# RetNet recurrence and SwiGLU block: first loads and steps in another order, the last token block in two halves, three w_out loads in two transfers

## The chip, the cores and the metric

The kernel runs on one core of a Trainium2 chip. The metric is the device time of one execution in microseconds. Five engines matter: TensorE (PE, with its weight loads PEld), VectorE (DVE), ScalarE (ACT), GpSimd (POOL) and SyncE (SP), which issues nearly all DMAs.

## The reference

```python
batch, n_heads, seq, head_dim = (4, 8, 768, 64)          # q, k, v, float32
n_tokens, d_model, d_ff = (3072, 512, 1536)              # w_gate, w_val: 512x1536, w_out: 1536x512

gamma = 1.0 - 2.0 ** (-5.0 - np.arange(H))
for t in range(S):
    state = gamma * state + outer(k[t], v[t])            # per batch and head
    y[t] = (1 / sqrt(D)) * q[t] @ state
x = y.transpose(0, 2, 1, 3).reshape(B * S, H * D)
g = x @ w_gate
out = (g * sigmoid(g) * (x @ w_val)) @ w_out
```

## The kernel before

**Tiling.** The sequence of each batch is cut into chunks of 128 tokens, and the heads are taken in four pairs. A chunk's contribution is a masked product of scores with v, plus a product of the decayed q with the state that the chunks before left. The work goes in four segments of six chunks (three positions of two batches). For each segment the attention output becomes x, then the two up products (w_gate, w_val) give h, then the down product with w_out gives six token blocks of 128 x 512 in six PSUM banks.

Products keep more than single precision's fast mode would: each operand is split in three parts (`near_a`, `near_b`, `near_c` at L960, L963, L966; `far_a`, `far_b`, `far_c` at L969, L399/L972, L976), and each product is three matmuls, one for each part. The weights come as 64-bit words and are converted on the chip to single precision (`convert_a` L532, L535, L538 on ScalarE, `convert_b` L545 and `convert_c` L553 on VectorE). Segment 0 keeps its converted weights in DRAM for the later segments, w_out's three parts in `w_dn3`.

**Order.** Nothing is scheduled by a framework. `PLAN` is one long string of names; `run` calls the step of each name in that order, so that the string sets each engine's instruction order. Every engine takes its instructions in order and waits at the head of its queue. The names of the start, with chunk numbers n from 0 to 5 (0 and 1 are the first chunks of two batches, 2 and 3 the second, 4 and 5 the third):

- `l n:w` loads k_t (w = 0), q_t (1), v (2) or k_n (3) of chunk n, 256 KB each (L464); q_t of chunks 0 and 1 is loaded on ScalarE's queue ahead of the plan. `A0`, `A1`, `A2` load the table: the two halves of the score mask and the decay factors (L586). `U`, `V` load weights (L511, 512 KB a matrix and block, in halves for block 0: gate with `U0:0`, val with `V0:0`).
- `s n` scores on TensorE (L628) and mask on VectorE (L634); `m n` masked scores times v (L713); `o n` decayed q times the old state (L699); `t n` the state's growth (L684), copied on ScalarE (L687) for chunks 0 and 1 or added on VectorE (L689); `g n` the state's decay (L670); `k n`, `q n` scale k_n and q on GpSimd (L649, L643), `K n`, `Q n` the same on VectorE; `x n:1`, `x n:2` split the attention output into x.
- `a`, `b`, `S`, `c`, `C` convert a weight block, one step after the other on ScalarE, ScalarE, VectorE, ScalarE, VectorE; `n f:i` makes the three parts of a weight block (0 to 2 gate, 3 to 5 val); `p f:j` and `v f:j` are the gate and val products for the chunk pair j of the first two blocks (L906), `u` and `y` the activation and product behind them; `G`, `W` the products of the later blocks (L888); `Z` keeps a converted block in DRAM.

The DMA completions use eight semaphores in turn: a load is issued when the one eight places earlier, over both queues, has landed.

**The end.** In a segment's down stage, `D f.tok` is the three matmuls of weight block f for token block tok (`down`, L1117 to L1122), `W f` loads the block's three parts from `w_dn3` (`w_load`, L1104), and `e tok` scales a token block out of its bank and stores it (`finish`, L1124 to L1143): odd blocks on VectorE (L1140), even ones on ScalarE (L1142), each stored through SP in one transfer. In the last segment block 5 is done in two halves, columns 0 to 255 on ScalarE (L1134) and 256 to 511 on VectorE (L1136). The last names of the plan are `3/D10.2 3/D11.2 3/e2`: token block 2 is the last.

Of the kernel before, what the change touches and what calls it, by code (L numbers as in the profile page):

```python
# [47 lines left out]


PLAN = """  # L50
    l1:0 A2 l0:0 A1 A0 l0:2 U0:0 l2:1 l0:3 s0 a0:1 l2:0 s1 m0 K0 b0:1 V0:0 S0:1 c0:1 l1:2 x0:2 s2
    l1:3 l3:0 x0:1 C0:1 l3:1 k1 U1:1 l2:3 t0 l2:2 l4:0 a0:0 g2 n0:0 Q2 l4:1 n0:1 m1 b0:0 S0:0 c0:0
    n0:2 t1 x1:1 a1:1 l3:3 x1:2 o2 C0:0 a1:0 s3 b1:1 S1:1 l3:2 q3 l5:1 n0:3 n0:4 c1:1 p0:0 l5:2 k2
    l5:0 o3 C1:1 m2 n0:5 t2 s4 b1:0 k3 v0:0 x2:2 S1:0 u0:0 g3 l4:2 U2:0 c1:0 m3 n1:0 U12:3 x2:1 t3
    C1:0 s5 q5 n1:1 h0 q4 o5 o4 x3:1 x3:2 m4 T0:0 n1:3 y0:0 T0:1 m5 p0:1 v0:1 a2 x4:1 u0:1 x5:2 U3:1
    n1:4 T1:0 y0:1 n1:2 T1:1 b2 p1:0 T0:2 U4:0 n1:5 u1:0 a12 Z0 p1:1 a3 x4:2 v1:0 x5:1 v1:1 y1:0
    p0:2 u1:1 v0:2 S2 U5:1 b12 c2 p1:2 u0:2 S12 T1:2 y1:1 C2 n2:0 n2:3 v1:2 y0:2 Z1 b3 n2:1 u1:2
    n2:2 S3 n2:4 T2:0 c3 a4 U13:2 G2:1 C3 y1:2 U6:0 T2:1 n3:0 G2:0 b4 n2:5 n3:1 i2:0 i2:1 T2:2 c12
    W2:0 j2:0 n3:2 W2:1 G3:1 n3:3 S4 C12 a5 Z2 j2:1 Z12 n3:4 c4 C4 U7:1 n3:5 T3:0 T3:1 c13 T3:2 G3:0
    n4:0 n4:1 b5 S5 n4:2 W3:0 n4:3 W3:1 i3:0 i3:1 n4:4 a13 a6 G4:1 c5 Z3 b13 G4:0 T4:0 U8:0 C5 T4:1  # L60
    j3:1 n4:5 b6 U14:3 W4:1 n5:0 T4:2 n5:1 i4:1 n5:2 n5:3 j3:0 S6 i4:0 a7 c6 n5:4 W4:0 T5:0 C6 G5:1
    Z4 T5:1 n6:0 L U9:1 j4:0 n5:5 S13 G5:0 a8 b7 n6:3 T5:2 j4:1 n6:1 c14 C13 W5:1 S7 i5:1 Z5 n6:4
    i5:0 n6:2 j5:1 c7 W5:0 G6:1 n6:5 l4:3 a9 U10:0 C7 n7:0 G6:0 j5:0 i6:1 T6:0 k4 b8 g4 Z13 n7:1
    n7:3 U15:2 S8 n7:2 W6:1 i6:0 c8 n7:4 T7:0 a14 W6:0 C8 l5:3 T7:1 T6:1 b14 G7:1 U11:1 n8:0 n8:1
    n7:5 i7:1 T6:2 G7:0 j6:0 b9 S14 W7:0 h2 c15 j6:1 Z6 S9 C14 n8:3 c9 n8:2 i7:0 n8:4 W7:1 G8:1 T7:2
    C9 G8:0 j7:0 n8:5 a10 b10 n9:0 j7:1 n9:3 Z14 a15 W8:0 P2 W8:1 Z7 n9:4 k5 b15 i8:0 S10 T8:0 n9:1
    i8:1 U16:3 n9:5 c10 S15 P0 T8:1 n9:2 C10 a11 C15 G9:0 t4 G9:1 P1 T9:0 i9:0 T8:2 Z15 j8:1 g5 j8:0
    t5 W9:1 W9:0 b11 n10:0 U17:2 T9:1 c16 Z8 n10:3 1/was0.0 a16 i9:1 n10:1 n10:4 n10:2 b16 G10:1 S11
    n10:5 c11 S16 i10:1 G10:0 0/h0.0 j9:0 C16 Z16 C11 n11:0 W10:0 n11:3 a17 j9:1 i10:0 0/h0.1 b17
# [299 lines left out]
def tile_retnet_swiglu(  # L369
# [747 lines left out]
    def down(f, tok):  # L1117
        i, u = divmod(tok, L)
        for a in range(3):
            nc.tensor.matmul(banks[tok], hs[f][:, a, ds(i * TH + u * P, P)], wo[f][:, a],  # L1120
                             start=f == a == 0, stop=f == NF - 1 and a == 2,
                             skip_group_check=True)  # L1122

    def finish(s, tok):  # L1124
        i, u = divmod(tok, L)
        p, pos = divmod(s * L, NCK)
# [4 lines left out]
        scale = ONE * ONE
        if s == NSEG - 1 and tok == 5:
            a, b = (ds(n * DM // 2, DM // 2) for n in range(2))
            act(t[:, a], banks[tok][:, a], AF.Copy, scale=scale)  # L1134
# [1 line left out]
            nc.vector.tensor_scalar(t[:, b], banks[tok][:, b], scale, None, op0=mul)  # L1136
            nc.sync.dma_start(out=out[ds(row, P), b], in_=t[:, b])
            return
        if tok % 2:
            nc.vector.tensor_scalar(t, banks[tok], scale, None, op0=mul)  # L1140
        else:
            act(t, banks[tok], AF.Copy, scale=scale)  # L1142
# [153 lines left out]
```

## Time and profile before

| | |
|---|---|
| runs | 643.41, 645.41, 645.75 us (median 645.41) |
| profiled execution | 643.87 us; span of its instructions 642.1 us |
| TensorE busy | 632.8 us of the span, granted clock 1.00 |
| TensorE's first real matmul | 6.67 us; its last wait ends at 16.79 us |
| TensorE's last matmul ends | 638.3 us |
| last store issued, landed | 638.96, 641.0 us |
| moved by DMA | 140.13 MB, 218 GB/s over the span |

A line of the chain of waits has the start in us, the length in us, and what the end waited for. A line of the timeline has the start, the length, the engine, the line of the program, the operation, the tiles written and read, how many instructions were merged, and in brackets the idle time before it and what ended that. A single-precision matmul appears in the timeline as two passes, so a step of eight matmuls is x16; the three-part products appear as one pass each.

### The profile page before, as it was taken

How to read it: one execution, taken by the hardware profiler on the slowest of the kernel's cores; microseconds unless marked ns; L12 is line 12 of the kernel's file. 1: busy time of each engine (PE TensorE's matmuls, PEld its weight loads, DVE VectorE, ACT ScalarE, POOL GpSimd, SP SyncE). 2: the span in 40 equal slices, each digit the busy share in tenths (PEclk: the TensorE clock that was granted, in tenths of full speed). 3: DMA queues.
4: the chain of work that ended last, by engine and by line, in shares of the span. 5: the costliest groups of instructions: out<-in, count | busy, mean ns of one | idle time of the engine just before them, and what ended most of it. 6: DMA issues, size and time to landing. Idle time of an engine off the chain costs nothing.

```text
span 642.1 us, 14098 instructions
## 1 busy us (share of the span) xinstructions
PE 632.8 (99%) x5576; PEld 580.2 (90%) x5576; DVE 487.8 (76%) x712; ACT 391.8 (61%) x860; POOL 264.5 (41%) x174
## 2 busy tenths in 40 slices
PE   7999999999999999999999999999999999999997
PEld 6899999987779999997778999998777999999886
DVE  4988887999898887665787869675789866778361
ACT  3678797777865565666766555564785555654121
POOL 0625555554436875630003665550101666653000
PEclk9999999999999999999999999999999999999999
DMA  9989988789787445258775640457767444304554
GB/s 320 375 290 338 317 320 290 281 290 328 259 283 298 170 151 173 69 171 270 248 240 213 198 164 8 183 196 247 241 223 264 155 163 173 115 0 157 195 184 170
DMA packets 50050, 140.13 MB, mean 218 GB/s; under 512 B 4928, under 2 KB 17472, under 8 KB 49984
## 3 DMA queue, kind: packets, MB, share of 16 engines
q1 hardware_dynamic: 49552, 138.57, 62.7%
q8 instruction: 44, 0.72, 0.5%
q10 hardware_dynamic: 432, 0.66, 0.3%
q14 instruction: 22, 0.18, 0.1%
HBM read 109.32 MB, written 29.88 MB: 217 GB/s over the span
## 4 chain that ended last, share of the span: by engine, by line
PE 97%; DMA 2%; SPq 0%; POOL 0%; ACT 0%; issue 0%; POOLq 0%
PE bank L1057 41%; PE bank L1120 32%; PE bank L888 13%; PE bank L758 6%; PE bank L906 3%; DMA hT<-in_k_n_dram 1%; DMA tab<-in_decays_dram 1%; PE bank L713 1%; PE bank L699 1%; PE bank L628 1%; PE bank L684 0%; POOL hT L649 0%; SPq L586 0%; SPq L464 0%; ACT chunk_x L1142 0%
## 5 line engine op out<-in xcount | busy, mean ns | idle before, releaser
L1120 PE MATMUL bank<-oitem,gitem 128*128 128x512 f32 x864 | 208.5, 395 | 0.0
L1120 PEld LDWEIGHTS bank<-oitem,gitem 128*128 128x128 f32 x864 | 159.0, 188 | 35.3 <-DMA oitem<-wdnt 0.5
L966 POOL TENSOR_TENSOR gitem<-gitem 128x768 fp32r<-128x768 f32 x72 | 140.6, 1963 | 116.6 <-DVE gitem L963 98.6
L1057 PE MATMUL bank<-xa,gitem 128*128 128x384 f32 x864 | 160.5, 334 | 0.0
L1057 PEld LDWEIGHTS bank<-xa,gitem 128*128 128x128 f32 x864 | 150.8, 188 | 0.2
L966 POOL TENSOR_TENSOR oitem<-oitem 128x256 fp32r<-128x256 f32 (+1 forms) x60 | 65.7, 1102 | 53.0 <-DVE oitem L963 51.2
L1057 PE MATMUL bank<-xb,gitem 128*128 128x384 f32 x432 | 84.5, 334 | 0.0
L888 PE MATMUL bank<-xa,oitem 128*128 128x384 f32 x480 | 84.4, 335 | 0.0
L888 PEld LDWEIGHTS bank<-xa,oitem 128*128 128x128 f32 x480 | 83.0, 188 | 0.4 <-DVE hT L442 0.2
L963 DVE SCALAR_TENSOR_TENSOR gitem<-gitem,loads 128x768 fp32r<-128x768 f32 x72 | 75.1, 1058 | 9.2 <-ACT gitem L960 7.8
L1057 PEld LDWEIGHTS bank<-xb,gitem 128*128 128x128 f32 x432 | 75.9, 188 | 0.4
L960 ACT ACTIVATE gitem<-loads 128x768 fp32r<-128x768 f32 x72 | 59.6, 843 | 25.9 <-PE bank L1057 16.8
L963 DVE SCALAR_TENSOR_TENSOR gitem<-gitem,hT 128x768 fp32r<-128x768 f32 x48 | 46.2, 965 | 25.4 <-ACT gitem L960 25.4
L960 ACT ACTIVATE gitem<-hT 128x768 fp32r<-128x768 f32 x48 | 40.2, 841 | 32.4 <-PE bank L1120 30.2
L991 ACT COPY chunk_x<-bank 64x128 f32<-64x128 f32 x144 | 36.6, 260 | 31.9 <-PE bank L758 21.1
L399 DVE SCALAR_TENSOR_TENSOR gitem<-gitem 128x768 fp32r<-128x768 f32 x48 | 49.1, 1030 | 0.8
L785 POOL TENSOR_TENSOR loads<-loads,tab 128x512 f32<-128x512 f32 x9 | 13.3, 1475 | 81.7 <-PE bank L758 44.6
L1057 PE MATMUL bank<-xb,oitem 128*128 128x384 f32 x216 | 43.4, 335 | 0.0
L1057 PEld LDWEIGHTS bank<-xb,oitem 128*128 128x128 f32 x216 | 38.0, 188 | 0.3
L1074 DVE TENSOR_TENSOR hT<-bank,tmp 128x384 f32<-128x384 f32 x36 | 20.0, 554 | 20.1 <-PE bank L1057 19.9
L963 DVE SCALAR_TENSOR_TENSOR oitem<-oitem,loads 128x256 fp32r<-128x256 f32 (+1 forms) x42 | 34.1, 816 | 0.9 <-ACT oitem L960 0.8
L1072 ACT COPY tmp<-bank 128x384 f32<-128x384 f32 x36 | 17.2, 478 | 27.9 <-PE bank L1057 18.9
(112 smaller groups left out, 792.3 us busy)
## 6 DMA issues: line engine op xcount, KB each, us to landing
loads<-wup SPq DMA_DIRECT2D x36, 896.0 KB, 4.7
oitem<-wdnt SPq DMA_DIRECT2D x36, 768.0 KB, 4.4
wdnt<-oitem SPq DMA_DIRECT2D x12, 768.0 KB, 5.9
wup<-first SPq DMA_DIRECT2D x9, 896.0 KB, 5.5
rawp<-in_w_gate_dram SPq DMA_DIRECT2D x12, 512.0 KB, 6.6
rawp<-in_w_val_dram SPq DMA_DIRECT2D x12, 512.0 KB, 6.2
rawp<-in_w_out_dram SPq DMA_DIRECT2D x12, 512.0 KB, 6.8
out_dram<-chunk_x SPq DMA_DIRECT2D x22, 256.0 KB, 2.2
```

The source lines that it names most:

```text
L399: stt(o, x, 1.0, y, op0=mul, op1=op)
L758: nc.tensor.matmul(o, a, b, start=start, stop=True, skip_group_check=True)
L888: nc.tensor.matmul(o, w[:, a, ts(b, P)], X0[:, a, i, NC - 1 - b], start=a == b == 0, stop=a == 2 and b == NC - 1, skip_group_check=True)
L906: nc.tensor.matmul(o, w[:, a, ts(b, P)], X0[:, a, :, NC - 1 - b, ts(j, P)], start=a == b == 0, stop=a == 2 and b == NC - 1, skip_group_che ...
L960: act(o[0], x, AF.Copy, scale=CUT / FAR)
L963: stt(o[1], f32(o[0]), -FAR, x, op0=mul, op1=add)
L966: op(o[2], f32(o[0]), f32(o[1]), op=add)
L991: copy(cx[half[i], ds(2 * h, 2), c, half[z]], y.rearrange("p (b t) -> p b t", b=2))
L1057: nc.tensor.matmul(o, w[:, a, k], x[:, a, KH - 1 - k], start=start and a == k == 0, stop=a == 2 and k == KH - 1, skip_group_check=True)
L1072: steps = (lambda: copy(p1, x), lambda: tt(c11, z, p1, op=add), lambda: act(gate, c11, AF.Silu, scale=ONE), lambda: copy(u2, x), lambda: c ...
L1074: lambda: copy(p5, wb), lambda: tt(h1, x, p5, op=add),
L1120: nc.tensor.matmul(banks[tok], hs[f][:, a, ds(i * TH + u * P, P)], wo[f][:, a], start=f == a == 0, stop=f == NF - 1 and a == 2, skip_group ...
```

## The change

It has four parts. The first 16 lines of `PLAN` (to about 100 us of the run) are written in another order, with the same names; the rest of the plan is as it was. The start of it before and after:

```diff
 PLAN = """
-    l1:0 A2 l0:0 A1 A0 l0:2 U0:0 l2:1 l0:3 s0 a0:1 l2:0 s1 m0 K0 b0:1 V0:0 S0:1 c0:1 l1:2 x0:2 s2
-    l1:3 l3:0 x0:1 C0:1 l3:1 k1 U1:1 l2:3 t0 l2:2 l4:0 a0:0 g2 n0:0 Q2 l4:1 n0:1 m1 b0:0 S0:0 c0:0
-    n0:2 t1 x1:1 a1:1 l3:3 x1:2 o2 C0:0 a1:0 s3 b1:1 S1:1 l3:2 q3 l5:1 n0:3 n0:4 c1:1 p0:0 l5:2 k2
-    l5:0 o3 C1:1 m2 n0:5 t2 s4 b1:0 k3 v0:0 x2:2 S1:0 u0:0 g3 l4:2 U2:0 c1:0 m3 n1:0 U12:3 x2:1 t3
-    C1:0 s5 q5 n1:1 h0 q4 o5 o4 x3:1 x3:2 m4 T0:0 n1:3 y0:0 T0:1 m5 p0:1 v0:1 a2 x4:1 u0:1 x5:2 U3:1
+    l0:2 l0:0 A1 A0 l1:0 U0:0 a0:1 s0 s1 l0:3 b0:1 l2:0 l2:1 S0:1 A2 K0 m0 c0:1 l1:3 C0:1 n0:0 l1:2
+    s2 V0:0 k1 l2:3 l2:2 Q2 t0 a0:0 l3:1 b0:0 m1 l3:0 U1:1 n0:1 x0:2 S0:0 o2 x0:1 c0:0 l4:0 l4:1
+    l3:3 t1 l3:2 m2 x1:1 C0:0 n0:3 k2 x1:2 g2 n0:4 t2 s3 a1:1 l5:1 b1:1 S1:1 n0:2 p0:0 x2:2 a1:0 q3
+    n0:5 k3 c1:1 g3 C1:1 b1:0 l5:0 v0:0 s4 S1:0 h0 l5:2 o3 m3 l4:2 t3 c1:0 C1:0 U2:0 x3:2 s5 u0:0 q5
+    x2:1 q4 U3:1 o5 o4 n1:0 x3:1 n1:1 n1:3 m4 n1:4 n1:2 m5 a2 T1:0 y0:0 U12:3 x5:1 x4:1 p0:1 u0:1 b2
...
```

So SP's queue begins, before, with k_t 1, A2, k_t 0, A1, A0, v 0, gate half 0, q_t 2, k_n 0, k_t 2, val half 0, v 1, k_n 1; and after with v 0, k_t 0, A1, A0, k_t 1, gate half 0, k_n 0, k_t 2, q_t 2, A2, k_n 1, v 1, val half 0, k_n 2, v 2. TensorE's first steps are s0, s1, m0, s2, t0, m1, t1, o2, s3, p0, o3, m2, t2, s4, v0, m3, t3, s5 before, and s0, s1, m0, s2, t0, m1, o2, t1, m2, t2, s3, p0, v0, s4, o3, m3, t3, s5 after.

In the last segment the loads of the w_out blocks 0, 1 and 2 go in two transfers, the first two parts (512 KB) and the third (256 KB). The last three matmuls of token block 2 become six, three for each half of the columns, and its scaling and store go in two halves, VectorE and SP for the first, ScalarE and its queue for the second:

```diff
             else:
-                nc.sync.dma_start(out=o, in_=w_dn3[f])
+                for i in (slice(2), slice(2, 3)) if s == NSEG - 1 and f < 3 else (slice(None),):
+                    nc.sync.dma_start(out=o[:, i], in_=w_dn3[f][:, i])
...
+    halves_of = [ds(n * DM // 2, DM // 2) for n in range(2)]
+    FINAL = 2
+
-    def down(f, tok):
+    def down(s, f, tok):
         i, u = divmod(tok, L)
-        for a in range(3):
-            nc.tensor.matmul(banks[tok], hs[f][:, a, ds(i * TH + u * P, P)], wo[f][:, a],
-                             start=f == a == 0, stop=f == NF - 1 and a == 2,
-                             skip_group_check=True)
+        final = s == NSEG - 1 and f == NF - 1 and tok == FINAL
+        for cols in halves_of if final else [slice(None)]:
+            for a in range(3):
+                nc.tensor.matmul(banks[tok][:, cols], hs[f][:, a, ds(i * TH + u * P, P)],
+                                 wo[f][:, a, cols], start=f == a == 0,
+                                 stop=f == NF - 1 and a == 2, skip_group_check=True)
...
+        if s == NSEG - 1 and tok == FINAL:
+            a, b = halves_of
+            nc.vector.tensor_scalar(t[:, a], banks[tok][:, a], scale, None, op0=mul)
+            nc.sync.dma_start(out=out[ds(row, P), a], in_=t[:, a])
+            act(t[:, b], banks[tok][:, b], AF.Copy, scale=scale)
+            nc.scalar.dma_start(out=out[ds(row, P), b], in_=t[:, b])
+            return
```

In the changed kernel's own numbering the two scalings of block 2 are L1147 (VectorE) and L1149 (ScalarE), and the products are L1126.

More of the change, by code (lines that the diff above doesn't have):

```diff
@@ L56 @@
[L56 to L66, printed above, removed]
+    l0:2 l0:0 A1 A0 l1:0 U0:0 a0:1 s0 s1 l0:3 b0:1 l2:0 l2:1 S0:1 A2 K0 m0 c0:1 l1:3 C0:1 n0:0 l1:2
@@ new lines @@
+    s2 V0:0 k1 l2:3 l2:2 Q2 t0 a0:0 l3:1 b0:0 m1 l3:0 U1:1 n0:1 x0:2 S0:0 o2 x0:1 c0:0 l4:0 l4:1
+    l3:3 t1 l3:2 m2 x1:1 C0:0 n0:3 k2 x1:2 g2 n0:4 t2 s3 a1:1 l5:1 b1:1 S1:1 n0:2 p0:0 x2:2 a1:0 q3
+    n0:5 k3 c1:1 g3 C1:1 b1:0 l5:0 v0:0 s4 S1:0 h0 l5:2 o3 m3 l4:2 t3 c1:0 C1:0 U2:0 x3:2 s5 u0:0 q5
+    x2:1 q4 U3:1 o5 o4 n1:0 x3:1 n1:1 n1:3 m4 n1:4 n1:2 m5 a2 T1:0 y0:0 U12:3 x5:1 x4:1 p0:1 u0:1 b2
+    T0:0 T1:1 v0:1 T0:1 y0:1 n1:5 p1:0 x4:2 T0:2 T1:2 p1:1 v1:0 u1:0 a3 a12 u1:1 x5:2 v1:1 U4:0 p0:2
@@ new lines @@
+    b12 y1:0 v0:2 p1:2 U5:1 S2 y1:1 S12 c2 Z1 u0:2 C2 n2:0 b3 y0:2 n2:1 u1:2 n2:3 v1:2 S3 y1:2 c3 Z0
+    n2:4 n2:2 T2:0 U13:2 G2:1 a4 C3 G2:0 n2:5 T2:1 U6:0 W2:0 i2:1 T2:2 n3:0 b4 i2:0 c12 a5 n3:1 n3:2
+    j2:0 W2:1 S4 n3:3 Z2 n3:4 c4 C12 c13 Z12 G3:1 j2:1 C4 U7:1 i3:1 n3:5 n4:0 T3:0 G3:0 i3:0 n4:1
+    n4:2 n4:3 T3:1 W3:1 a13 b5 T3:2 G4:1 Z3 a6 n4:4 S5 c5 j3:1 W3:0 C5 n5:0 n4:5 G4:0 b6 b13 T4:0
+    T4:1 n5:1 L U8:0 T4:2 n5:3 U14:3 n5:2 i4:1 j3:0 S6 n5:4 W4:1 a7 W4:0 c6 i4:0 T5:0 C6 G5:1 c14
@@ L67 @@
+    n6:0 n5:5 Z4 S13 j4:1 T5:1 G5:0 n6:3 a8 W5:1 j4:0 T5:2 U9:1 n6:1 n6:2 n6:4 C13 Z5 b7 W5:0 i5:1
+    j5:1 S7 n6:5 U10:0 G6:1 i5:0 c7 C7 a9 j5:0 l4:3 G6:0 T6:0 i6:1 n7:0 b8 n7:3 g4 W6:0 l5:3 n7:1
+    Z13 U15:2 n7:2 S8 W6:1 c8 T6:1 i6:0 a14 b14 n7:4 n7:5 T7:0 G7:1 C8 T7:1 U11:1 G7:0 i7:1 n8:0
+    j6:0 n8:3 S14 W7:0 n8:1 b9 T6:2 c15 j6:1 n8:4 i7:0 S9 Z6 k4 n8:2 h2 W7:1 C14 c9 G8:1 T7:2 C9
+    G8:0 j7:0 n8:5 a10 b10 n9:0 j7:1 n9:3 Z14 a15 W8:0 P2 W8:1 Z7 n9:4 k5 b15 i8:0 S10 T8:0 n9:1
     i8:1 U16:3 n9:5 c10 S15 P0 T8:1 n9:2 C10 a11 C15 G9:0 t4 G9:1 P1 T9:0 i9:0 T8:2 Z15 j8:1 g5 j8:0
@@ L1132, in finish @@
         if s == NSEG - 1 and tok == 5:
-            a, b = (ds(n * DM // 2, DM // 2) for n in range(2))
+            a, b = halves_of
             act(t[:, a], banks[tok][:, a], AF.Copy, scale=scale)
@@ L1137, in finish @@
             nc.sync.dma_start(out=out[ds(row, P), b], in_=t[:, b])
+            return
+        if s == NSEG - 1 and tok == FINAL:
+            a, b = halves_of
+            nc.vector.tensor_scalar(t[:, a], banks[tok][:, a], scale, None, op0=mul)
+            nc.sync.dma_start(out=out[ds(row, P), a], in_=t[:, a])
+            act(t[:, b], banks[tok][:, b], AF.Copy, scale=scale)
+            nc.scalar.dma_start(out=out[ds(row, P), b], in_=t[:, b])
             return
@@ L1191, in down_stage @@
             tok = b
-            at(t, f"{s}/D{f}.{tok}", down, f, tok)
+            at(t, f"{s}/D{f}.{tok}", down, s, f, tok)
             t += 3 * PASS_D
```

## The prediction

> **What bounds the kernel now.** I read four views: the page's busy shares, the chain of waits, the timeline of TensorE's start, and the timeline of the tail.
>
> ```profile
> PE 632.8 (99%) x5576; PEld 580.2 (90%) x5576; DVE 487.8 (76%) x712; ACT 391.8 (61%) x860; POOL 264.5 (41%) x174
> ...
> PE 97%; DMA 2%; SPq 0%; POOL 0%; ACT 0%; issue 0%; POOLq 0%
> ```
>
> TensorE is the bound. In the chain nothing but TensorE stands between 16.79 and 638.32 us:
>
> ```profile
> 2.59 5.46 DMA tab<-in_decays_dram
> 8.05 0.02 issue
> 8.06 7.49 DMA hT<-in_k_n_dram
> ...
> 15.69 1.05 POOL hT L649
> 16.75 0.04 issue
> 16.79 0.69 PE bank L684 x16
> ...
> 32.80 14.59 PE bank L906 x120
> ...
> 590.66 47.66 PE bank L1120 x210
> 638.32 0.02 issue
> 638.34 0.60 ACT chunk_x L1142
> ```
>
> So time can be won or lost only before 16.79 and after 638.3, unless the new order opens a hole in between. TensorE's start:
>
> ```profile
> 6.67 3.63 PE L628 MATMUL bank<-hT 64*128 64x128 f32 x32 [1.80 <-DMA hT<-in_k_t_dram]
> 10.22 1.09 PE L713 MATMUL bank<-tmp,hT 128*64 128x128 f32 x16
> 12.84 1.16 PE L628 MATMUL bank<-hT 64*128 64x128 f32 x16 [1.52 <-DMA hT<-in_k_t_dram]
> 13.93 0.69 PE L684 MATMUL bank<-hT 128*64 128x64 f32 x16
> 14.92 1.09 PE L713 MATMUL bank<-tmp,hT 128*64 128x128 f32 x16 [0.30 <-DMA hT<-in_v_n_dram]
> ```
>
> These are s0 and s1, m0, s2, t0, m1. TensorE waits for loads four times; the last wait ends at 16.79, for the k_n of chunk 1 and the GpSimd scaling behind it. Where the last wait ends, with the work already done by then, sets everything after it.
>
> **The loads.** Each landing in the trace follows the one before it by 0.68 us per 256 KB (k_n of chunk 0 at 12.02, k_t of 2 at 12.71, v of 1 at 14.88, k_n of 1 at 15.56); a 512 KB weight half takes 1.49 (val half 0, at 14.20) to 1.95 (gate half 0, at 10.66). The first eight landings are at 4.49, 4.67, 5.55, 5.87, 6.54, 7.37, 8.05, 8.71. An issue waits until the load eight earlier has landed (the gate half was issued at 4.68, chunk 0's q_t landed at 4.67). So a load's landing follows from its place in the queue.
>
> **Part 1, the new start.** By the new queue order: k_t 0 takes the landing at 5.55, table halves A1 and A0 6.54 and 7.37, k_t 1 8.05; then the gate half 9.5 to 10.0 (one place earlier, so issued 1.6 us earlier), k_n 0 10.2 to 10.7, q_t 2 about 12.0, the late table part A2 12.7, k_n 1 13.4, v 1 14.1, val half 15.6, k_n 2 16.2, v 2 16.9. Against before, k_n 1 is 2.2 us earlier, v 1 0.8, while A2 is 7 us and the val half 1.4 us later.
>
> TensorE in the new order: s0 at 5.6 to 7.3, s1 8.1 to 9.8 (both at the pace of the 32 passes in 3.63), m0 to 10.9, s2 12.0 to 13.1. t0 needs K0 on VectorE (0.69, L649), which needs A2: 13.4, so t0 runs 13.5 to 13.95; m1 14.1 to 15.2. o2 needs Q2; VectorE has in front of it K0 to 13.4, C0:1 (0.68), two masks (1.29) and Q2 (0.84) itself: o2 at about 16.15, where before it began at 17.41. Then t1 17.2, m2 17.65 to 18.65. t2 writes the bank that ScalarE copies after t1, and that copy is queued behind the val half's conversion: L532 at 15.65 (0.70), L535 (0.60), x1:0 (0.58), then L538, which waits for VectorE's Q2, L963, L976 and L545 (0.69 each, to 18.05), so L538 ends at 18.75 and the copy (0.36) at 19.1. So t2 starts at 19.15, with the wait moved there from t1. After it stand t2 0.69, s3 1.09, p0 and v0 1.62 each, s4 1.09, o3 and m3 1.02 each, t3 0.47, s5 1.09, o4 and o5 1.89, m4 and m5 1.90 (durations from the chain of waits): 13.50. The long L906 run begins at 32.65, against 32.80: **-0.15**. The stall went from k_n 1 to the conversion of the val half, which the change moved back behind k_n 1 and v 1.
>
> Bounds: if ScalarE's copy is free in time, t2 follows m2 at 18.65: -0.65. If the val half takes the 1.95 of the gate half, or another 0.6 us is lost ahead of it, everything on that chain moves: +0.45.
>
> The remaining reordering up to 130 us (weight loads, their splits and conversions on SP, VectorE, ScalarE, GpSimd) I cost at 0. What covers it is TensorE's queue of L906 and L888 products: none of its waits in the trace falls after 16.79. There the helpers wait for TensorE, not it for them (the waits view has ScalarE's L442 behind L888 for 3.3 us and GpSimd's L555 behind L888 for 4.4). If that cover failed once, by one 512 KB load out of place, it would cost 1.5.
>
> **Part 2, the tail.**
>
> ```profile
> 636.11 0.38 ACT L1134 ACTIVATE tmp<-bank 128x256 f32<-128x256 f32 x1
> 636.52 0.42 DVE L1136 TENSOR_SCALAR tmp<-bank 128x256 f32<-128x256 f32 x1 [2.93 <-ACT tmp L1134]
> ```
>
> This is the other block that is already scaled in halves: the second half had to wait for the first, though they write different columns. The built order of the changed kernel says the same of the new block: ScalarE's half (L1149) waits for VectorE's, and VectorE's (L1147) for the one count that TensorE gives after all six new products. So the halves run one after the other, after the last product. Six 128x256 products at 14.59/120 = 0.122 are 0.73 against three 128x512 at 47.66/210 = 0.227, 0.68: +0.05. Then 0.42 + 0.03 + 0.38 takes the place of 0.60: +0.23. The last store is 128 KB on ScalarE's queue, 2.1 us to landing, against 256 KB on SP's, 2.2 over the kernel and 2.04 for this one: between -0.1 and +0.1, I take 0. **+0.3.** Bounds: +0.4, and -0.25 if the first half were scaled under the products of the second (0.38 in place of 0.60, and the store's -0.1).
>
> **Part 3, w_out.** In the last segment blocks 0, 1, 2 land at 582.44, 590.41, 594.93, and their first products start at 588.07, 592.58, 596.66: 5.6, 2.2 and 1.7 us of cover. Three more issues cost SP 0.32 each and the second transfer lands perhaps 0.7 later (one 256 KB landing step), while only the third product of a group reads it, 0.46 after the first. **0**; with the cover gone 0.7 at most, and no gain, since nothing waits there.
>
> **Sum**: -0.15 + 0.3 + 0 = +0.15, so 644.0 against the profiled execution's 643.87 (span 642.1, 1.77 around it). The runs shown are 643.41, 645.41 and 645.75; with the profiled one, two of four lie near 643.6 and two near 645.6, and the median of the four is 644.64. For a measurement over several runs I therefore put **644.8**; on the median of the three alone it would be 645.6.
>
> **Rivals.**
>
> (a) *TensorE stays slow for longer, so slower.* In the trace the first 32 passes of L628 took 3.63 us, and later 16 take 1.16: the early ones go at 1/1.6 of the pace, and full pace came during the unbroken run from 6.67 to 11.3. The new start breaks that run: s0, a hole of 0.8, s1 and m0 for 2.8, a hole of 1.1, then pieces of 1 to 2 us until 16.15. If the slow pace lasts until 3.4 us of unbroken work have passed, o2, t1 and m2 (2.5 us) take 4.0, t2 starts at 20.15 (+1.0) and the next 3.4 us do 2.1 us of work (+1.3): +2.3 on the sum, 647.1. For it: the holes, and the two levels of the runs before, which may be this. Against: before, too, there was a hole of 1.8 us ahead of 6.67, and slow pieces fill their own holes. It decides from the point where t2 starts later than 19.15; to cost 3.2 us the slow pace would have to last past 25 us. The Trainium skill's "TensorE: Matmul & The Clock Gate", Part 1, has this as a rule: half rate until a free-running window of about 3.4 us was busy. By that rule the start could come out either way from run to run; the trace agrees in that the granted clock was full from 10.0, 3.3 us into the unbroken run.
>
> (b) *The halves do overlap and ScalarE is free in time*: -0.65 - 0.25, so 643.7. Against: the built order's waits.
>
> (c) *A hole opens after 32 us*: a weight load or its conversion is late once for 1.5 to 4 us: 646.3 to 648.8. For: the DMA engines are full until 33 us (share 1.05 to 1.08 in the stretches) and the weight loads behind them change places. Against: the waits view has no wait of TensorE there.
>
> (d) *The load order matters more than I see*, another 1.5 us at the start: 642.9. Against: v of chunk 5 stays last and lands at the same 27.4, and VectorE's and ScalarE's chains to t2 have no such slack.
>
> **Chances.** Forecast 0.50, (a) 0.25, (b) 0.10, (c) 0.10, (d) 0.05. The range takes in (a), (b), (d) and the scatter: 642.9 to 647.1; the likeliest case alone, with the two levels of the runs, 643.4 to 645.9. 0.5% is 3.2 us, about what a measurement of this kernel can tell from no change: faster by that needs most of (d) twice over, 0.04; slower by that takes the upper end of (c), or (a) past 25 us, 0.08; within it 0.88.
>
> **What would show it.** Right: t2's L684 is the last TensorE start with a wait, at about 19.1, and waits for ScalarE; s1 starts near 8.1, o2 near 16.1; the L906 run starts at 32.4 to 32.8; L1149 starts 0.45 after L1147. Wrong: passes of L628 or L713 still at the slow pace after 13 us; a TensorE wait after 33 us; L1147 starting before TensorE's last product; the first products of the last segment waiting for oitem.

## The result, and the profile after

The changed kernel takes 647.32 us (median of 12 runs, 645.59 to 649.66) against 644.66 for the kernel before (12 runs beside it): ratio 1.0042, interval 1.0027 to 1.0058. Run again beside other runs of the kernel before it was 1.0021 (1.0007 to 1.0035). So it is slower, by 0.42% in the one comparison and 0.21% in the other, whose intervals overlap; the 647.32 us lie above the predicted range by 0.2 us. The profiled execution took 646.7 us, its span 644.6 against 642.1.

TensorE's work is the same, 633.2 us against 632.8. The page of the changed kernel shows that less of the chain runs through TensorE:

```profile
PE 633.2 (98%) x5579; PEld 580.7 (90%) x5579; DVE 485.2 (75%) x713; ACT 393.1 (61%) x860; POOL 267.4 (41%) x174
...
PE 90%; DMA 5%; DVE 2%; ACT 1%; issue 1%; SPq 1%; POOL 0%; ACTq 0%; DVEq 0%; POOLq 0%
```

TensorE had 97% of the chain before. The 2.5 us between the two profiles are three pieces: the long run of L906 products begins at 33.5 in place of 32.7 (+0.8); waits and small gaps in TensorE's run after that add 2.0; the end is 0.3 shorter (3.48 us from the last product to the end of the span, 3.78 before).

TensorE's start in the changed kernel (timeline; in brackets the idle time before, and what ended it):

```profile
8.62 2.05 PE L628 MATMUL bank<-hT 64*128 64x128 f32 x16 [2.06 <-DMA hT<-in_k_t_dram]
10.61 1.80 PE L713 MATMUL bank<-tmp,hT 128*64 128x128 f32 x16
12.34 1.16 PE L628 MATMUL bank<-hT 64*128 64x128 f32 x16
...
16.72 1.09 PE L699 MATMUL bank<-loads,states 64*64 64x128 f32 x16 [1.15 <-DVE loads L643]
...
20.28 0.69 PE L684 MATMUL bank<-hT 128*64 128x64 f32 x16 [0.98 <-POOL oitem L966]
```

s1 (8.62) and m0 go at little more than half pace: 2.05 us against the 1.16 of s2, which has as many passes, and 1.80 against 1.09 for m0 in the kernel before. The granted clock reads 0.50 from 9 to 12 us. o2 starts at 16.72 and t2 at 20.28. The bracket of t2 names GpSimd, but the last thing it needs is ScalarE's copy, which the timeline of the other engines has at the end of a queue:

```profile
16.22 1.25 POOL L649 TENSOR_TENSOR hT<-hT,tab 128x512 f32<-128x512 f32 x1 [1.37 <-DMA hT<-in_k_n_dram]
16.49 1.53 DVE L963 SCALAR_TENSOR_TENSOR oitem<-oitem,first 128x512 fp32r<-128x512 f32 x1
...
19.26 0.68 ACT L538 ACTIVATE first<-rawp 128x512 int32<-128x512 uint32 x1 [1.84 <-DVE bank L545]
...
19.84 0.35 ACT L687 COPY states<-bank 128x256 f32<-128x256 f32 x1
```

L963 takes 1.53 us in place of 0.69: it began while GpSimd's L649 was running and ended 0.55 after it. In a0, the changed kernel run again, it starts before L649 (15.82):

```profile
15.32 0.69 DVE L963 SCALAR_TENSOR_TENSOR oitem<-oitem,first 128x512 fp32r<-128x512 f32 x1
```

The stretch that was covered before, in the chain of waits of the changed kernel (start, length, what; most pieces of 0.05 us and less are left out):

```profile
41.11 10.61 DMA wup<-first
51.73 0.03 ACT first L532
...
52.77 0.48 ACT tmp L442
53.31 6.79 DMA rawp<-in_w_gate_dram
60.13 0.04 ACTq L538
...
61.25 1.13 ACT rawp L538
62.38 0.27 ACT tmp L442
62.69 0.64 ACT oitem L960
63.36 0.70 DVE oitem L963
...
64.19 1.35 POOL oitem L966
65.58 24.48 PE bank L888 x138
```

Read from the top: the store Z0 of the converted block 0 lands at 51.7 (42.7 before). ScalarE's L532 (a4) writes into the stored tile and waits for it; the weight load U6:0 may only overwrite what a4 has read, so it is issued at 52.9 and 53.3 (50.5 and 50.9 before) and lands at 60.1 (57.1). The next conversion c4 (L538) reads the tile that U6:0 writes and stands behind it in `PLAN`, so it waits for the landing; behind c4 in ScalarE's queue stand c13, a copy, and then the L960 that makes the next part for TensorE. TensorE waits at 63.38 (0.78 over the usual time between two products), at 65.58 (0.68), and once more at 136.84 (0.65). In the kernel before, ScalarE waits for the same landing, but 3 us earlier, and TensorE's run of L888 products goes through (timeline of the kernel before):

```profile
47.75 24.43 PE L888 MATMUL bank<-xa,oitem 128*128 128x384 f32 x140
...
57.16 1.14 ACT L538 ACTIVATE first<-rawp 128x1024 int32<-128x1024 uint32 x1 [1.51 <-DMA rawp<-in_w_gate_dram]
```

The tail of the changed kernel (timeline):

```profile
641.21 0.42 DVE L1147 TENSOR_SCALAR chunk_x<-bank 128x256 f32<-128x256 f32 x1 [0.70 <-PE bank L1126]
641.67 0.38 ACT L1149 ACTIVATE chunk_x<-bank 128x256 f32<-128x256 f32 x1 [2.33 <-DVE chunk_x L1147]
642.08 0.35 ACTq L1150 DMA_DIRECT2D out_dram<-chunk_x  x1
```

The halves go one after the other, but the last store lands at 643.81, 1.72 after its issue (2.04 before).

### The profile page after: what moved, and what is told of

The parts are those of the page before. It is cut to its first block, busy times and chain, and to the rows that moved or that the text cites. A ratio compares the mean times of both kernels' runs of the same rounds, so it can differ in the third digit from the quotient of the medians.

```text
span 644.6 us, 14110 instructions
## 1 busy us (share of the span) xinstructions
PE 633.2 (98%) x5579; PEld 580.7 (90%) x5579; DVE 485.2 (75%) x713; ACT 393.1 (61%) x860; POOL 267.4 (41%) x174
## 4 chain that ended last, share of the span: by engine, by line
PE 90%; DMA 5%; DVE 2%; ACT 1%; issue 1%; SPq 1%; POOL 0%; ACTq 0%; DVEq 0%; POOLq 0%
PE bank L1057 41%; PE bank L1126 32%; PE bank L888 10%; PE bank L758 6%; DMA wup<-first 2%; DMA rawp<-in_w_out_dram 1%; DMA rawp<-in_w_gate_dram 1%; DMA hT<-in_k_t_dram 1%; PE bank L628 1%; PE bank L906 0%; POOL oitem L966 0%; DVE tmp L634 0%; SPq L511 0%; DVE oitem L963 0%; PE bank L684 0%
## 5 line engine op out<-in xcount | busy, mean ns | idle before, releaser
L1126 PE MATMUL bank<-oitem,gitem 128*128 128x512 f32 x867 | 208.0, 394 | 0.5 <-DVE hT L442 0.5
L1126 PEld LDWEIGHTS bank<-oitem,gitem 128*128 128x128 f32 x867 | 159.6, 188 | 34.8 <-DVE hT L442 0.8
L966 POOL TENSOR_TENSOR gitem<-gitem 128x768 fp32r<-128x768 f32 x72 | 142.1, 1983 | 115.3 <-DVE gitem L963 97.3
L888 PE MATMUL bank<-xa,oitem 128*128 128x384 f32 x480 | 85.1, 336 | 1.1 <-ACT oitem L960 0.6
L888 PEld LDWEIGHTS bank<-xa,oitem 128*128 128x128 f32 x480 | 82.9, 188 | 2.4 <-ACT oitem L960 0.9
L963 DVE SCALAR_TENSOR_TENSOR gitem<-gitem,loads 128x768 fp32r<-128x768 f32 x72 | 75.6, 1064 | 10.7 <-ACT gitem L960 9.3
L960 ACT ACTIVATE gitem<-loads 128x768 fp32r<-128x768 f32 x72 | 59.7, 843 | 25.9 <-PE bank L1057 16.7
L963 DVE SCALAR_TENSOR_TENSOR gitem<-gitem,hT 128x768 fp32r<-128x768 f32 x48 | 46.5, 972 | 26.7 <-ACT gitem L960 26.7
L960 ACT ACTIVATE gitem<-hT 128x768 fp32r<-128x768 f32 x48 | 40.3, 844 | 33.4 <-PE bank L1126 30.5
L399 DVE SCALAR_TENSOR_TENSOR gitem<-gitem 128x768 fp32r<-128x768 f32 x48 | 47.7, 1002 | 0.8
L963 DVE SCALAR_TENSOR_TENSOR oitem<-oitem,loads 128x256 fp32r<-128x256 f32 (+1 forms) x42 | 35.1, 839 | 3.4 <-ACT oitem L960 3.3
```

The costliest lines, as they stand in the source:

```text
L399: stt(o, x, 1.0, y, op0=mul, op1=op)
L888: nc.tensor.matmul(o, w[:, a, ts(b, P)], X0[:, a, i, NC - 1 - b], start=a == b == 0, stop=a == 2 and b == NC - 1, skip_group_check=True)
L960: act(o[0], x, AF.Copy, scale=CUT / FAR)
L963: stt(o[1], f32(o[0]), -FAR, x, op0=mul, op1=add)
L966: op(o[2], f32(o[0]), f32(o[1]), op=add)
L1126: nc.tensor.matmul(banks[tok][:, cols], hs[f][:, a, ds(i * TH + u * P, P)], wo[f][:, a, cols], start=f == a == 0, stop=f == NF - 1 and a = ...
```

## The experiments

"Run" is the start of the long L906 run; "waits" are those of TensorE between 50 and 100 us: the time between two products over the median for that pair of shapes, where over 0.12. Both come from one profile each, and so does "last product to end"; the ratio goes by 6 to 12 runs against 12 to 35 of the kernel before.

| kernel | ratio (interval) | run | waits | last product to end |
|---|---|---|---|---|
| before | 1 | 32.73 | 0.00 | 3.78 |
| changed | 1.0042 (1.0027 to 1.0058) | 33.53 | 1.46 | 3.48 |
| a0, changed again | 1.0021 (1.0007 to 1.0035) | 32.00 | 1.70 | 3.48 |
| e3 tail alone | 0.9998 (0.9987 to 1.0009) | 33.16 | 0.66 | 3.67 |
| e6 start alone | 0.9996 (0.9986 to 1.0005) | 33.54 | 0.00 | 3.78 |
| e10 middle alone | 1.0013 (1.0002 to 1.0025) | 32.94 | 0.61 | 3.78 |
| e13 new order to m5 | 0.9995 (0.9983 to 1.0008) | 32.93 | 1.31 | 3.48 |
| e14 new order to Z0 | 1.0023 (1.0012 to 1.0034) | 33.62 | 0.80 | 3.48 |
| e4 U12:3 behind, in before | 1.0006 (0.9989 to 1.0022) | 33.95 | 0.55 | 3.79 |
| e11 Z0 behind, in before | 1.0016 (1.0004 to 1.0028) | 32.71 | 1.21 | 3.79 |
| e16 both behind, in before | 1.0010 (0.9996 to 1.0024) | 33.99 | 1.82 | 3.79 |
| e1 changed, U12:3 back | 1.0008 (0.9995 to 1.0022) | 32.94 | 2.05 | 3.48 |
| e9 changed, Z0 back | 1.0018 (1.0004 to 1.0031) | 32.83 | 3.28 | 3.48 |
| e15 changed, both back | 1.0004 (0.9993 to 1.0015) | 33.09 | 0.87 | 3.47 |
| e2 changed, copy free | 1.0016 (1.0003 to 1.0030) | 32.27 | 1.58 | 3.48 |
| e12 both back, copy free | 0.9995 (0.9976 to 1.0013) | 31.83 | 1.63 | 3.48 |
| e7 changed, warm-up | 1.0042 (1.0024 to 1.0059) | 33.63 | 0.79 | 3.47 |
| e17 start, copy free, tail | 0.9997 (0.9986 to 1.0009) | 33.49 | 0.00 | 3.68 |
| e18 changed, U13 behind U6 | 1.0051 (1.0031 to 1.0071) | 33.28 | 2.55 | 3.48 |
| e19 as e12, U13 behind U6 | 1.0033 (1.0021 to 1.0046) | 32.13 | 1.61 | 3.49 |

The waits of one profile explain the time only in part: e13 and e12 have 1.31 and 1.63 us of them at no loss in time, e7 has 0.79 at +0.42%. The column also stops at 100 us. Behind 200 us, where all these kernels run the same plan, TensorE waits in some profiles for a load from `w_dn3`, near 312 us, by the same measure 1.18 us in e4 and in e16, 1.04 in e10, 0.89 in e6, and not at all in before, changed, e7, e12 and e15. What makes that wait long or short is open.

### The tail (e3)

The kernel before with the last block in halves, as in the diff of `down` and `finish`.

> The kernel before with the last token block in halves and nothing else. The prediction had +0.3 us for it (halves scaled one after the other, the store taken as equal). The traces of the two kernels read the other way: from TensorE's last product to the end of the span 3.42 us against 3.78, its six products 0.03 longer. If the traces are right the time is 0.3 us below the kernel before (-0.05%), the two scalings stand one behind the other, and the last store (128 KB on ScalarE's queue) lands in 1.7 us. If the prediction is right: +0.3 us, with a store of 2.0 to 2.1.

Measured: no difference in time. The profile has the halves one behind the other and the last store landing 1.74 after its issue: the traces' reading holds, the predicted +0.3 is not there. From the last product to the end it is 0.1 shorter; the kernels that also load w_out in two transfers are 0.3 shorter.

### The start (e6, e2, e7)

e6 is the kernel before with the new order up to t2; e2 moves one name of the changed kernel, e7 adds one:

```diff
-... o2 x0:1 c0:0 l4:0 l4:1 l3:3 t1 l3:2 ...
+... o2 x0:1 l4:0 l4:1 l3:3 t1 c0:0 l3:2 ...
```
```diff
-... a0:1 s0 s1 l0:3 ...
+... a0:1 s0 w12 s1 l0:3 ...
+        "w": lambda n: warm_up(n),
```

> The kernel before with the new order only for the start (up to t2) and the old order from there on; tail and w_out loads as before. Theory: the start alone costs what the trace of the changed kernel shows there: t2 at 19.5 to 20.3, the L906 run at 33.2 to 33.6 in place of 32.8, and no wait of TensorE near 63 us, because the stores and weight loads stand as before: +0.4 to +0.8 us, +0.1%. Rival: the new start is what delays the weight stream too; then waits of over 0.5 us near 63 us come here as well and the time is +0.3% or more.

> The changed kernel with ScalarE's step c0:0 (L538, which waits for VectorE's conversion of the val half) moved behind t1, so that the copy L687 after t1 is no longer queued behind it. Theory: t2 waits for that copy alone; the copy can start when t1 ends, at 18.2, so t2 starts at 18.6 to 19.3 in place of 20.28, and the L906 run begins at 32.5 to 32.9 in place of 33.53. The hole in the loads and the waits near 63 us stay, so the time is 0.7 to 1.0 us below the changed kernel's: +0.25% against the kernel before. Rival: TensorE's slow clock up to 12.1 us, not the copy, set the start; then t2 follows something else at 20 and the L906 run stays at 33.4 or later, time +0.4%.

> The changed kernel with 12 more warm-up matmuls (their result is used by nothing) between s0 and s1, where TensorE would stand idle for a load. In the profiles of the new start the granted clock fell to 0.50 for about 3.4 us at 7 to 9 us in five of eight, and stayed full in three. Prediction's rival (a), the slow clock costs the start: here the clock stays full from 5 to 15 us, s1 to m1 take 1.1 us or less each, and the L906 run begins 0.5 to 1 us earlier than the 32.8 to 33.6 of the changed kernel's profiles with a drop; time 0.1% below the changed kernel's. Other theory (loads and VectorE's chain to the copy set t2, the slow passes fill holes): the L906 run begins at 32.0 to 33.6 as with no warm-up, time +0.2 to +0.4% as for the changed kernel.

Measured: e6 has the same late run as the changed kernel's profile and no wait behind it:

```profile
48.04 27.21 PE L888 MATMUL bank<-xa,oitem 128*128 128x384 f32 x156
```

One unbroken run across 63 us; the time is that of the kernel before. In e2 t2 starts at 18.42 and the run at 32.27, as expected; that the waits behind it are 1.58 is taken up below. In e7 the passes up to s2 go at full pace, and the slow ones come at t0 and m1 instead:

```profile
9.40 1.16 PE L629 MATMUL bank<-hT 64*128 64x128 f32 x16
10.49 1.09 PE L714 MATMUL bank<-tmp,hT 128*64 128x128 f32 x16
...
14.77 1.12 PE L685 MATMUL bank<-hT 128*64 128x64 f32 x16 [1.84 <-DVE hT L650]
15.68 1.91 PE L714 MATMUL bank<-tmp,hT 128*64 128x128 f32 x16
```

(its lines are one higher). The granted clock stays at 1.00 to 14 us and is 0.51 from 16 to 18, so the slow stretch came later and did not go away. Nothing is gained: t2 starts at 20.39 and the run at 33.63.

### Which part of the order makes TensorE wait (e10, e13, e14)

e10 is the kernel before up to s5 and the new order from there; e13 and e14 are the changed kernel with the old order from behind m5, and from behind Z0.

> The kernel before up to s5 (TensorE's last scores, about 28 us), from there on the new order; tail and w_out loads as before. So far the waits of TensorE between 30 and 100 us (time between two products over the usual, above 0.12) are 1.5 to 2.1 us in the changed kernel and in it with one load moved, 3.3 with the store moved ahead, 0.0 to 0.7 in kernels with the old order, and 0.0 with the new start alone. Theory M (the order of the middle costs it, whatever the start): waits of 1.2 us or more between 55 and 70 us come here too, time +0.2 to +0.3%. Rival S (it takes the new start as well, that is, the late weight load U3:1 behind it): no wait above 0.7 near 63 us, within 0.1%.

> The new order up to m5 (the last step ahead of TensorE's long run of products, about 33 us), from there on the old order; tail and w_out loads as before. Theory M (the order behind m5: conversions, stores and copies from 33 us on): no wait above 0.7 between 55 and 70 us, time within 0.1% of the kernel before. Rival S (what stands between t2 and m5 in the new order, U12:3 behind U3:1 and the conversions there): the waits of 1.2 us or more near 63 us are here, +0.2%.

> The new order up to Z0 (the store of block 0, issued at about 41 us), from there on the old order; tail and w_out loads as before. If the cause lies between m5 and Z0 (the conversions a3 and a12 ahead of U4:0, both stores behind U5:1): waits of 1.2 us or more near 63 us as in the changed kernel, +0.2%. If it lies behind Z0 (ScalarE's a4 and b4 ahead of what TensorE needs next): no wait above 0.7 there, within 0.1%.

One correction: e13 and e14 had the new tail and the new w_out loads, not the old ones as their expectations say. Measured: neither theory wins. Waits come with each part (0.61, 1.31 and 0.80), no part alone has what the whole order has. By the times the step from e13 (0.9995) to e14 (1.0023), intervals apart, lies in the names from m5 to Z0. The waits of their two profiles do not bear it out: e13 has more of them than e14.

### Two suspects, taken back and put in (e1, e4, e9, e11, e15, e16, a0)

U12:3 is the first w_out load, which needs nothing; in the new order it stands on SP behind U3:1, whose issue waits for ScalarE until 29.5. Z0 is the store of block 0; in the new order it stands behind U5:1 and Z1. e1 and e9 move one each in the changed kernel, e15 both:

```diff
-... q4 U3:1 ... T1:0 y0:0 U12:3 x5:1 ... U4:0 p0:2 ... c3 Z0 n2:4 ...
+... q4 U12:3 U3:1 ... T1:0 y0:0 x5:1 ... U4:0 Z0 p0:2 ... c3 n2:4 ...
```

e4 and e11 make one of the moves each the other way in the kernel before, e16 both:

```diff
-... n1:0 U12:3 x2:1 ... x5:2 U3:1 n1:4 ... a12 Z0 p1:1 ... y0:2 Z1 b3 ...
+... n1:0 x2:1 ... x5:2 U3:1 U12:3 n1:4 ... a12 p1:1 ... y0:2 Z1 Z0 b3 ...
```

> The changed kernel with one name moved: the first w_out load U12:3, which needs nothing, stands again ahead of the weight load U3:1, whose issue waits for ScalarE's conversion L538. Theory A (the hole in the loads): in the changed kernel SP stood at U3:1 until 29.49 us with U12:3 behind it, the DMA engines ran at a share of 0.75 from 25 to 33 us (1.07 in the kernel before), and all weight loads behind came 2.6 to 4.7 us later, which ended in TensorE's waits of 0.78, 0.68 and 0.65 at 63.4, 65.6 and 136.8 us. Then here the share of 25 to 33 us is about 1.05, the landings after 33 us are 2 to 4 us earlier, those three waits are gone or below 0.2, and the span is 1.5 to 2 us shorter than the changed kernel's 644.6; against the kernel before the time is +0.1% (+0.5 us). Rival B (the other order of the conversions and of the stores wup behind it, not this load): the share of 25 to 33 us is mended but the waits at 63 and 65 us stay, time as the changed kernel, +0.4%. The start stays as in the changed kernel: the L906 run begins at about 33.5.

> The kernel before with the suspected cause put in alone: the w_out load U12:3 moved behind the weight load U3:1 on SP's queue, everything else as before. Theory A (the hole in the loads): the DMA share of 25 to 35 us falls below 0.9, later weight loads land 2 us or more later than in the kernel before, and TensorE gets waits of together 1 to 1.5 us near 63 us: the time rises by 1 to 1.5 us (+0.15 to +0.25%). Rival B: the load has slack enough there, nothing moves, within 0.1%.

> The changed kernel with one name moved: Z0, the store of the converted block 0, stands again right behind the weight load U4:0 and ahead of U5:1, as in the kernel before, in place of behind Z1. Theory C (the store): in the changed kernel Z1 and Z0 were issued back to back at 40.6 and 41.1 and Z0 landed at 51.7 (42.7 in the kernel before); ScalarE's L532, which writes into the stored tile, waited for it, U6:0 was issued 2.4 later, its load landed at 60.1, and TensorE waited 0.78 and 0.68 for what comes out of it. Then here Z0 lands before 46, the load of U6:0 lands 2 us or more earlier, the two waits at 63 and 65 us are gone and the time is 1.4 us (0.2%) below the changed kernel's of this call. Rival B (the order of the conversions on ScalarE and VectorE sets it): the waits stay, no change in time.

> The kernel before with the suspected cause put in alone: Z0, the store of block 0, moved behind U5:1 and Z1, everything else as before. Theory C: Z0 is issued at about 43.8 and lands at 50 or later, ScalarE's L532 waits for it, U6:0 is issued 2 us or more later, and TensorE gets waits of together 1 to 1.5 us near 63 us: +0.15 to +0.25% against the kernel before. Rival B: the loads run 2 us earlier there than in the changed kernel, so the store has slack: no wait above 0.3 near 63 us, within 0.1%.

> The changed kernel once more, unaltered, on the chip and against the runs of the kernel before that the next three share. Its first comparison gave +0.42% (interval +0.27 to +0.58), while the changed kernel with one load moved (e1) and with one ScalarE step moved (e2) gave +0.08% and +0.16% on another day, though their traces kept the waits of TensorE at 62 to 65 us. If those two moves did little and the measurement scatters from chip to chip, this is about +0.15%; if they each bought most of it back, this is +0.4%. In the trace the waits at 63, 65 and 136 us, the start of the L906 run at 33.2 to 33.6 and the DMA share of 0.75 from 25 to 33 us come again, since the order of every queue is the same.

> The changed kernel with two names moved back: U12:3 ahead of U3:1 and Z0 right behind U4:0; nothing else. Two-cause theory: put into the old order alone the two cost +0.06% and +0.16%, so here their sum of 0.2% (1.4 us) goes and only the start and the tail are left: -0.05% against the kernel before, with the waits of TensorE from 30 to 100 us below 0.7 us. Rival (the conversions' order behind Z0): the waits stay at 1.5 us or more and the time at +0.15% or more.

> The kernel before with the same two put in together: U12:3 behind U3:1 and Z0 behind Z1; nothing else. Two-cause theory: +0.2 to +0.25% against the kernel before, with waits of TensorE of 1.2 us or more from 30 to 100 us. Rival (the conversions' order costs it, and the +0.16% of the store alone was scatter): below +0.1%, waits below 0.7 us.

Measured: no single theory holds in all of its traces. The stretch of 25 to 33 us, in the kernel before, in the changed kernel and in e1 (busy time of PE, PEld, DVE, ACT, POOL, then granted clock, DMA share, GB/s):

```profile
25.00:33.00 8.00, 8.00 (x126) 7.33 (x126) 7.90 (x14) 4.63 (x13) 4.77 (x5) 1.00 1.07 371
```

```profile
25.00:33.00 8.00, 8.00 (x139) 7.30 (x139) 6.92 (x12) 5.37 (x13) 2.52 (x2) 1.00 0.75 241
```

```profile
25.00:33.00 8.00, 8.00 (x141) 7.17 (x137) 7.05 (x12) 5.13 (x12) 2.51 (x3) 1.00 1.07 371
33.00:45.00 12.00, 12.00 (x102) 12.00 (x101) 11.84 (x21) 8.57 (x13) 3.39 (x2) 1.00 0.75 237
```

e1 fills the hole of 25 to 33 us and the same hole opens at 33 to 45; the waits stay. The hole alone does not make them: e15 has it at 33 to 45 too (share 0.71). e9 lands Z0 at 44.3, but now Z1 is late (51.2), and the waits grow. With both back, e15 is at 1.0004 (the changed kernel 1.0042 and 1.0021), and of the pair of waits at 63 and 65 us its profile has 0.21 left, as the two-cause theory says. By the times it is not told from the rival that one move is enough: e1 alone is at 1.0008, within e15's interval. The other way the theory holds by half: e11 and e16 bring waits of 1.2 and 1.8, and e11 has the time expected of it (+0.16%), but its waits lie at 69 and 78 us, and e16's time, +0.10% (-0.04 to +0.24), is less than the 0.2% expected, with 1.18 us of its profile lost at 314 us.

### The start is given back (e12, e17)

e12 is e15 with e2's move as well; e17 is the kernel before with the new start, e2's move in it, and the tail.

> The changed kernel with three names moved at once: U12:3 ahead of U3:1, c0:0 behind t1, Z0 behind U4:0, so that SP's queue stands from U12:3 on as in the kernel before. If the order of the loads and stores on SP's queue is the cause, each move alone having left another part of it (the late issue of U3:1, the late landing of Z0), then the waits near 63 us fall below 0.7, the L906 run begins at 32.0 to 32.6, and with the shorter tail the time is 0 to 0.1% below the kernel before. If the order of the conversions on ScalarE and VectorE is the cause, the waits of 1.2 us or more stay and the time is +0.1 to +0.2%.

> The kernel before with only the parts that should gain: the new start up to t2 with c0:0 behind t1, the old order from there on, and the last block in halves. With the copy free, t2 came at 18.6 to 19.3 and the L906 run at 31.8 and 32.3 in the two profiles that had this (32.7 to 34.0 with the old start): -0.5 to -1.0 us; the tail -0.3 us or, by e3's time, nothing. Theory: -0.1 to -0.2% against the kernel before, no wait above 0.7 near 63 us. Rival (an earlier start is given back at 63 us, because the weight stream does not come earlier): waits of 0.5 to 1 us there, time within 0.05%.

Measured: e12 keeps the order of e15 on SP and yet waits 1.12 at 61 and 63 us. Its run begins 1.26 earlier than e15's, but U6:0 lands only 0.2 earlier (58.07 against 58.27): TensorE comes sooner to a part that does not. e17 has no waits between 50 and 100 us, but its run begins at 33.49, behind the expected 31.8 to 32.3 although t2 starts at 18.95: at 24.16 TensorE waits 0.84 for a mask (L634) on VectorE, whose L963 took the long 1.53. The time is that of the kernel before.

### The load itself (e18, e19)

Set against the start of the run, the landing of U6:0's second half orders the eighteen profiles so far: up to 24.9 us behind it no kernel waits between 50 and 67.5 us; from 25.2 on those with the new order behind Z0 do, 1 us more for each us. (Those with the old order there have some 0.6 us more room: 0.00 at 25.44 in e14, 0.45 at 26.08 in e13, 0.50 at 26.11 in e16.) To see whether the load is the cause, the 1 MB of U13:2 ahead of it was put behind it:

```diff
-... T2:0 U13:2 G2:1 a4 C3 G2:0 n2:5 T2:1 U6:0 W2:0 ...
+... T2:0 G2:1 a4 C3 G2:0 n2:5 T2:1 U6:0 U13:2 W2:0 ...
```

> The changed kernel with one name moved: the w_out load U13:2 (1 MB) behind the weight load U6:0 in place of ahead of it; every conversion, store and product in its old place. Theory L (the landing of U6:0 against TensorE's progress): without the 1 MB ahead of it the gate half of U6:0 lands 2 us or more earlier, about 56 to 57 us, 23.5 to 24.5 after the start of the L906 run in place of 26.6 to 26.9; the waits of TensorE at 55 to 75 us fall from 1.5 to 1.7 us to below 0.4, and the time by 1.2 us or more against the changed kernel: 0 to +0.15% against the kernel before. Rival (the conversions' order): the load lands earlier, but the waits of 1.2 us or more stay, and the time at +0.2 to +0.4%. A third way: U13:2, now 4 us later, is waited for itself at 100 us or later.

> The changed kernel with four names moved: U12:3, c0:0 and Z0 as in e12, and U13:2 behind U6:0. In e12 the L906 run began at 31.8, 0.9 earlier than in the kernel before, and TensorE gave it back in waits of 1.1 us at 61 and 63 us, the gate half of U6:0 landing 26.2 after the run's start. Theory L: here it lands 23.5 to 24.5 after the start, those waits are below 0.4, and start (up to -0.9) and tail (-0.3) are kept: -0.1 to -0.2% against the kernel before. Rival: waits of 1 us there as in e12, time within 0.05%.

Measured: U6:0 lands 2.1 us earlier (24.5 behind the run's start in e18, 26.6 in the changed kernel), but the waits before 67.5 are 2.14, not below 0.4: the third way, and earlier than expected. ScalarE's timeline of e18:

```profile
57.87 1.14 ACT L538 ACTIVATE first<-rawp 128x1024 int32<-128x1024 uint32 x1 [0.69 <-DMA rawp<-in_w_gate_dram]
61.76 1.11 ACT L538 ACTIVATE rawp<-rawp 128x1024 int32<-128x1024 uint32 x1 [2.76 <-DMA rawp<-in_w_out_dram]
...
63.14 0.62 ACT L960 ACTIVATE oitem<-first 128x512 fp32r<-128x512 f32 x1
```

c4 runs at 57.87, and then c13, which needs U13:2, stands at the head of ScalarE's queue until that lands (61.68), with TensorE's L960 behind it. c13 comes 1.05 after c4, so the later of "U6:0 landed" and "U13:2 landed, less 1.05" is what counts. With the order of the changed kernel behind Z0 (us after the run's start; waits of TensorE from 50 to 67.5 us):

| kernel | U6:0 landed | U13:2 landed - 1.05 | waits |
|---|---|---|---|
| e15 | 25.18 | 19.74 | 0.21 |
| e10 | 25.24 | 20.43 | 0.27 |
| e7 | 25.55 | 19.93 | 0.59 |
| e12 | 26.24 | 20.00 | 1.12 |
| e19 | 23.66 | 26.32 | 1.14 |
| e2 | 26.48 | 20.45 | 1.16 |
| changed | 26.58 | 20.58 | 1.46 |
| a0 | 26.91 | 20.85 | 1.70 |
| e1 | 27.00 | 19.40 | 1.88 |
| e9 | 27.19 | 20.02 | 2.06 |
| e18 | 24.48 | 27.35 | 2.14 |

The wait is the larger of the two numbers less 25.0, within 0.35, in all eleven. This rule was read off these profiles, its second column only after e18; no further run tests it. The kernel before has 24.33. So by it the kernel before had little more than a microsecond of room at one place, and the new order used it up: 0.6 by what stands behind Z0, the rest by a later issue (Z0; 1.6 in the changed kernel) and a longer way of the load (6.8 us against 6.2; 8.4 in e1), or by an earlier start of TensorE.

## Why the prediction was wrong

**Part 1, the start.** "The long L906 run begins at 32.65, against 32.80", so -0.15. One profile says +0.8, but the profiles scatter: 32.00 to 33.62 in nine with the new start (mean 33.08), 32.71 to 33.99 in six with the old one (mean 33.25). On the mean the change is -0.16, give or take 0.3 by the scatter of these fifteen, so it is not told from nothing, and that it falls on the predicted -0.15 is luck; as a bound +0.45 was too narrow for a single execution. The chain to t2 was the right one (val half's conversion, L538, the copy L687), and e2 shows it: with L538 out of the way t2 starts at 18.42. Two of its terms were missed. ScalarE's L535 of the first conversion waits for the mask of s1, which uses the same bank (1.44 us in the changed kernel); and L963 takes 1.53 when it begins while L649 runs. Both go with the pace of the first passes: of the fourteen profiles with the new start, s1 takes 1.88 to 2.08 in the ten where L963 takes 1.53 to 1.55, and 1.16 to 1.65 in the other four. So that part of rival (a) was real: in a0, with all passes at full pace, L963 is at 15.32, ahead of L649, and t2 at 18.30; in the eight other profiles with that start t2 is at 19.58 to 20.37, where rival (a) had 20.15. The further 1.3 us that it put behind t2 did not come: from 12.34 on the changed kernel's products go at full pace. What a start at full pace throughout is worth was not measured: e7 only moved the slow passes, and a0, which had it by chance, gave it back in waits of 1.70.

**The reordering up to 130 us, "I cost at 0".** This is the step that failed. Its reason, "There the helpers wait for TensorE, not it for them", was read from totals of waits over the whole stretch. A helper may wait 3 us for TensorE at one product and have 1 in hand at the next; the conversions c4 and c13, waiting for loads at the head of ScalarE's queue ahead of TensorE's L960, had that little. Rival (c) had the mechanism and the price (1.5 to 4 us, "a weight load or its conversion is late once"), at a chance of 0.10, and was set aside on the same ground, that no wait showed before the change. Gaps and waits from 30 to 200 us are 2.5 and 2.6 in the two profiles of the changed kernel and 0.6 on the mean in before, e3, e4 and e6: +1.9.

**Part 2, the tail, +0.3.** The order of the halves was right; the sign was not. "I take 0" for the store was the mis-sized term: the 128 KB store lands in 1.72 to 1.74 against 2.04, which pays for the scalings one after the other (the last store is issued 0.91 behind the last product, 0.66 before). e3 alone is at no difference in time and 0.1 shorter at the end in its profile, the whole change 0.3 shorter.

**Part 3, the w_out loads, 0.** No wait was seen there. That the end is 0.2 shorter only where these loads are split (0.84 from the last landing to the end of the span in the nine such profiles that have this landing, 1.02 and 1.03 in e3 and e17) was not foreseen, and its cause is open.

**The sum.** -0.16 + 1.9 - 0.3 = +1.4 us, 0.22%: what the second comparison measures (+0.21%); the first, +0.42%, leaves 1.3 us that these means do not show. The sum leaves out what is lost behind 200 us.

**What stays open.** That the order behind the start costs the time is shown (the start and the tail alone cost nothing, and taking two moves back gives the time back); which names of it do so is shown by half. The two moves of e15 bring the changed kernel back to the time of the kernel before (its interval lies apart from that of the first comparison of the changed kernel and overlaps the second's); put into the old order they cost half of what was expected. No version was faster than the kernel before beyond the measurement; e13, e12 and e17 are within it.

## What to carry to other kernels

That the bound engine shows no waits does not mean that there is slack: before moving a load, a store or a conversion, follow the shortest chain from it to the next product (store landed, tile free, load issued, load landed, conversion, part) and write down its margin at that one place. An earlier start is only worth something if the stream of loads behind it has that much room; otherwise it comes back as a wait. And a full DMA queue is best looked at as a whole: taking one transfer back moved the hole by 10 us and left the waits (e1), taking two back left 0.21 of the pair at 63 and 65 us (e15).

## What the hardware showed that was not expected

- VectorE's L963 (two SBUF inputs) takes 0.69 alone or when it starts ahead of GpSimd's L649 (a0: 15.32 against 15.82). When it starts while L649 is running, 0.04 (e13) to 0.30 us (e6) behind its start, it takes 1.53 to 1.55. The Trainium skill, "SBUF — State Buffer", section "SBUF: two separate sides", has a rule for it: such an operation and one of GpSimd that reads SBUF hold one port pair in turn, and the later one is blocked for the whole of the earlier. The trace agrees: 17.47, where L649 ends, plus 0.55 is the end of L963, and it ends 0.55 behind L649 in the nine other profiles with the long L963 too. In e12, where L963 starts 0.16 ahead, it is L649 that takes longer, 1.43 against the 1.04 of the kernel before.
- Two stores of 896 KB issued 0.5 us apart among loads took 9.0 and 10.6 us to land (changed kernel, from 40.6); issued 5.6 us apart 4.9 and 5.5 (kernel before). The distance is not all of it: in e11 two such stores issued 0.4 us apart took 5.7 and 7.3. The DMA engines were busy meanwhile: shares of 0.82 to 1.05 from 41 to 49 us of the changed kernel, moving 239 to 425 GB/s.
- With the same order s1 and m0 took 2.05 and 1.80 us in one execution (changed kernel, granted clock 0.50 from 9 to 12 us) and 1.16 and 1.09 in another (a0, granted clock 1.00), and the long run began 1.5 us apart.
